# The 640-point column DFTs of a spectral filter as 10-point butterflies on VectorE and 64-point products on TensorE

## The chip, the cores and the metric

The kernel runs on one core of a Trainium2 chip. The metric is the device time of one execution in microseconds (us). Of most kernels several executions are taken, and the median is quoted with the lowest and the highest; all of these were in the fast state. e2, e3 and e7 are single runs, so their state is unknown; their times are used with care, their instruction durations more freely. The granted TensorE clock was 1.0 to within 0.002 except in e4 (0.97) and e6 (0.96 to 0.97). The span of a profile is 1.7 to 3.0 us shorter than the time of the same execution.

In the profiles PE is the matrix unit (TensorE), PEld its weight loads, DVE VectorE and ACT ScalarE. `arena` is the program's memory in SBUF, from which the matmuls read; `ps` is PSUM, into which they write. "L926" is line 926 of that kernel's source; lines shift between the kernels, so the names of the stages are given beside them.

## The reference

Shortened:

```python
def reference(A_x, A_w_r, A_w_i, B_x, B_w_gate, B_w_up, B_w_down):   # x: 1 x 2048 x 640, bf16
    def _A_ref(x, w_r, w_i):                       # w_r, w_i: 2048 x 321
        X = rfft2(x.astype(float32)) * (w_r + 1j * w_i)
        return irfft2(X, s=(S, D)).astype(bfloat16)
    def _B_ref(x, w_gate, w_up, w_down):           # 640 x 1536, 640 x 1536, 1536 x 640
        return ((x @ w_gate) * (x @ w_up)) @ w_down
    xn = _layernorm(A_x, axis=-1)
    return A_x + _A_ref(xn, A_w_r, A_w_i) + _B_ref(xn, B_w_gate, B_w_up, B_w_down)
```

So there is a layernorm, then two branches on its result: a gated network, and a filter in the two-dimensional frequency domain. The sum of both and the input is the output.

## The kernel before

The program is a list of small tasks, each with an engine, a price in ns and a priority. A planner simulates the engines with these prices when the kernel is built, and fixes the order of instructions on each engine. Each engine then runs its list in order; before's trace shows it at 107.02 us, where a gate product on DVE had waited 0.27 us for ACT, and CB (L935), whose operands WM had finished at 106.76, ran only after it, at 107.23. A price that is wrong changes nothing in the work, only in the order.

The stages, each done for 16 blocks or tiles of 128 rows:

- **LN**: layernorm of a 128 x 640 block; statistics, subtraction and scale on DVE. The block is transposed on PE.
- **GU, eG, H**: the gated products (ten matmuls a unit), their eviction on ACT, and the product gate times up on DVE. They depend only on LN and fill PE wherever the filter waits.
- **L1, L2**: the folds that cut the 640-point column DFT into even and odd, cosine and sine halves, on DVE.
- **R**: first half of the 2048-point row DFT. **D**: the column DFT, with the folded cosine and sine matrices. **C**: second half of the row DFT (complex, four matmuls).
- **WM, CB**: the spectral product with the weights (DVE, PSUM times SBUF), and its combination into real and imaginary part.
- **IA, IB**: first half of the inverse row DFT. **I**: the inverse column DFT. **U1, U2**: its unfolding on DVE.
- **ACC, FIN**: down-projection, with the second half of the inverse row DFT as a thirteenth matmul into the same sum; then the addition of the input on DVE, and the store.

The parts that the argument touches (prices, dependencies and the first lines of the functions cut, comments added):

```python
# D: the column DFT of one tile
for h in range(2):
    c.e.matmul(ps[:, bk + h, 0:320], v_uq[:, 4, t, :], v_fd[:, 640 + 320 * h: 960 + 320 * h], start=True, stop=False)
    for g in (2 * h, 2 * h + 1):
        o = (g % 2) * 160
        ins = c.e.matmul(ps[:, bk + h, o:o + 160], v_uq[:, g, t, :], v_fd[:, g * 160:(g + 1) * 160],
                         start=False, stop=(g % 2 == 1))
# WM: the spectral product. p (fp32) = x (PSUM, fp32) * weights (SBUF, bf16); e = even or odd column
x4 = ps[:, bk:bk + 2, 0:_LP].rearrange("p c (e m) -> p c e m", e=2)
for w in range(2):
    wv = v_w[:, wr, w, :].rearrange("p (m e) -> p e m", e=2)
    wv = wv.unsqueeze(1).to_broadcast([128, 2, 2, 161])
    ins = c.e.tensor_tensor(v_p[:, r2, w, :, :].rearrange("p c (m e) -> p c e m", e=2), x4, wv, _OP.mult)
# CB
c.e.tensor_tensor(v_y[:, r2, 0, :], v_p[:, r2, 0, 0, :], v_p[:, r2, 1, 1, :], _OP.subtract)
c.e.tensor_tensor(v_y[:, r2, 1, :], v_p[:, r2, 0, 1, :], v_p[:, r2, 1, 0, :], _OP.add)
```

The innermost loop of WM runs over m. In SBUF the weights are then read at every second bf16 (a step of 4 bytes) and the product is written at every second fp32 (8 bytes).

Of the kernel before, what the change touches and what calls it, by code (L numbers as in the profile page):

```python
# [70 lines left out]
class _Sched(object):  # L71
# [81 lines left out]
    def plan(self, nbanks=8, filler_deadline=0.0):  # L153
# [56 lines left out]
        while nsch < ntot:  # L210
            cands = []
            for t in avail:
# [14 lines left out]
                for ei, e in enumerate(t.engs):  # L227
                    est = eng_free[e]
                    for d in t.deps:
                        lat = _SLAT[e] if d.eng == e and not d.nbytes else _XLAT[e]  # L230
                        de = d.end + lat
                        if de > est:
                            est = de
                    if bank_ready > est:
                        est = bank_ready
                    fin = est + t.dur[e]
                    score = fin + (self.affinity if ei > 0 else 0.0)
                    if best is None or score < best[3]:
                        best = (est, fin, e, score)
# [153 lines left out]
def _build_tables():  # L393
# [25 lines left out]
    dd = np.arange(160) + 0.5  # L419
    lset = (np.arange(0, 320, 2), np.arange(1, 321, 2), np.arange(2, 322, 2), np.arange(1, 321, 2))  # L420
    full = []
    for g in range(4):
        ang = two_pi * dd[:, None] * lset[g][None, :] / _D
        full.append(np.cos(ang) if g < 2 else -np.sin(ang))
    fd = np.zeros((128, 4 * 160 + 640), np.float64)
    for g in range(4):
        fd[:, g * 160:(g + 1) * 160] = full[g][0:128]
        fd[g * 32:(g + 1) * 32, 640 + g * 160:640 + (g + 1) * 160] = full[g][128:160]
    t["fd"] = _bf16_bits(fd)

    gd = np.zeros((128, 4 * 160 + 640), np.float64)
    ml = np.arange(128)
    for g in range(4):
        l_ = 2 * ml + (g % 2)
        cl = np.where((l_ == 0) | (l_ == 320), 1.0, 2.0) / _D
        ang = two_pi * l_[:, None] * dd[None, :] / _D
        gd[:, g * 160:(g + 1) * 160] = cl[:, None] * (np.cos(ang) if g < 2 else -np.sin(ang))
        l_ = 256 + 2 * np.arange(33 if g % 2 == 0 else 32) + (g % 2)
        cl = np.where(l_ == 320, 1.0, 2.0) / _D
        ang = two_pi * l_[:, None] * dd[None, :] / _D  # L440
        v = cl[:, None] * (np.cos(ang) if g < 2 else -np.sin(ang))
        if g == 0:
            v[32] = 0.0
        gd[l_ - 256, 640 + g * 160:640 + (g + 1) * 160] = v
# [11 lines left out]
    ti = np.zeros((128, 16, 2, 256), np.float64)  # L456
    for tt in range(16):
# [18 lines left out]
        ti[:, tt, 0, 0:128] = im.real.T  # L476
        ti[:, tt, 0, 128:256] = im.imag.T
        ti[:, tt, 1, 0:128] = -im.imag.T
        ti[:, tt, 1, 128:256] = im.real.T
# [21 lines left out]
_CHUNKS = ((0, 1), (1, 1), (2, 1), (3, 1), (4, 2), (6, 2), (8, 2), (10, 2), (12, 2), (14, 2))  # L501
_LP = 322
# [36 lines left out]
def _build(nc, A_x, A_w_r, A_w_i, B_w_gate, B_w_up, B_w_down, out, opts=None):  # L539
# [3 lines left out]
    with es:  # L543
# [8 lines left out]
        sch.caps = {"glu": opts.get("cap_glu", 2), "acc": opts.get("cap_acc", 3), "fill": 1}  # L552
# [17 lines left out]
        b_w = alloc("W", _NW * 2 * _LP)  # L570
        b_z2 = alloc("Z2", 3 * 2 * 2048)
        b_x = alloc("X", 16 * 640, at=lay["Z2"][0])
        b_tf = alloc("TF", 16 * 3 * 128)
        b_ti = alloc("TI", 16 * 512)
        b_wd = alloc("WD", 12 * 640, at=lay["TI"][0])
        b_fd = alloc("FD", 1280)
        b_g = alloc("G", 1280)
# [3 lines left out]
        b_dum = alloc("DUM", 256)  # L581
        o_r = cur[0]

        b_l = alloc("L", 2 * 1280)
        b_f = alloc("F", 3 * 640)
# [4 lines left out]
        b_y = alloc("Y", 2 * 2 * _LP)  # L590
        o_end = max(o_end, cur[0])
        cur[0] = o_r
        b_tc = alloc("TC", 2 * 640)
        b_pm = alloc("PM", 2 * 1280)
# [18 lines left out]
        v_v = V("V").rearrange("p (a d) -> p a d", a=16)  # L613
        v_w = V("W").rearrange("p (r w l) -> p r w l", r=_NW, w=2)
        v_z2w = V("Z2").rearrange("p (tc a t m) -> p tc a t m", tc=6, a=16, t=16)
        v_z2 = V("Z2").rearrange("p (t c a n) -> p t c a n", t=3, c=2, a=16)
        v_x = V("X").rearrange("p (r d) -> p r d", r=16)
        v_tf = V("TF").rearrange("p (t m k) -> p t m k", t=16, m=3)
# [5 lines left out]
        v_gbf = V("GBF").rearrange("p (r n) -> p r n", r=6)  # L624
        v_dum = V("DUM")
        v_l = V("L").bitcast(_F32).rearrange("p (r c d) -> p r c d", r=2, c=2)
        v_ff = V("F").rearrange("p (r n) -> p r n", r=3)
        v_fm = v_ff[:, :, 0:512].rearrange("p r (g d) -> p r g d", g=4)
        v_fr = v_ff[:, :, 512:640].rearrange("p r (g d) -> p r g d", g=4)
        v_a = V("A").rearrange("p (r n) -> p r n", r=3)  # L630
        v_p = V("P").bitcast(_F32).rearrange("p (r w c l) -> p r w c l", r=2, w=2, c=2)
        v_y = V("Y").rearrange("p (r c l) -> p r c l", r=2, c=2)
        v_tc = V("TC").bitcast(_F32).rearrange("p (r c d) -> p r c d", r=2, c=2)
        v_pm = V("PM").bitcast(_F32).rearrange("p (r s c d) -> p r s c d", r=2, s=2, c=2)
# [8 lines left out]
        v_rs = SF(448, 16)  # L643
        v_mv = arena[:, o_stat + 384: o_stat + 416].rearrange("p (b k) -> p b k", b=16)
# [5 lines left out]
        b_rs = sch.buf("rs", 10 ** 9 + 20, 1)  # L650
        b_sd = sch.buf("sd", 10 ** 9 + 30, 1)
# [29 lines left out]
        dma("ld_fd", v_fd, d_fd, 128 * 2560, [(b_fd, None)], prio=0.3)  # L681
# [3 lines left out]
        dma("ld_g", v_g, d_g, 128 * 2560, [(b_g, None)], prio=0.36)  # L685
# [33 lines left out]
        for gi, (b0, nb) in enumerate(_LN_GROUPS):  # L719
            pbase = (1.0 if gi < 4 else 5.4) + 0.05 * gi  # L720
            for b in range(b0, b0 + nb):
                def em_bn(c, b=b):
                    c.e.bn_stats(v_st[:, b, 0:6], v_x[:, b, 0:320])  # L723
                    return c.e.bn_stats(v_st[:, b, 6:12], v_x[:, b, 320:640])
                T("bn%d" % b, "dve", 800.0, em_bn, reads=[(b_x, ("s", b, b + 1))],
                  writes=[(b_st, ("b", b, b + 1))], prio=pbase)

                def em_ag(c, b=b):
                    return c.e.bn_aggr(v_mv[:, b, :], v_st[:, b, :])
                T("ag%d" % b, "dve", 130.0, em_ag, reads=[(b_st, ("b", b, b + 1))],  # L730
                  writes=[(b_mv, ("b", b, b + 1))], prio=pbase)
# [15 lines left out]
            for b in range(b0, b0 + nb):  # L747
# [7 lines left out]
                def em_mul(c, b=b):  # L755
                    return c.e.tensor_scalar(v_x[:, b, :], v_x[:, b, :], v_rs[:, b:b + 1], None, _OP.mult)
                muls[b] = T("mul%d" % b, "dve", 290.0, em_mul, reads=[(b_rs, ("b", b, b + 1))],
# [21 lines left out]
        for b in range(16):  # L779
            lr = b % 2  # L780
            fr = b % 3
            pf = 6.0 + 0.05 * b

            def em_l1(c, b=b, lr=lr):
                c.e.tensor_tensor(v_l[:, lr, 0, :], v_x[:, b, 0:320], v_x[:, b, 639:319:-1], _OP.add)
                return c.e.tensor_tensor(v_l[:, lr, 1, :], v_x[:, b, 0:320], v_x[:, b, 639:319:-1], _OP.subtract)  # L786
            T("L1_%d" % b, "dve", 2 * _d_dve(320), em_l1, after=[muls[min(b + 6, 15)]],
              reads=[(b_x, ("s", b, b + 1))],
              writes=[(b_l, ("r", lr, lr + 1))], prio=pf)

            def em_l2(c, lr=lr, fr=fr):
                ins = None
                for v_, lo, n in ((v_fm, 0, 128), (v_fr, 128, 32)):
                    c0 = v_l[:, lr, :, lo:lo + n]
                    c1 = v_l[:, lr, :, 319 - lo:319 - lo - n:-1]
                    c.e.tensor_tensor(v_[:, fr, 0:4:3, :], c0, c1, _OP.add)  # L796
                    ins = c.e.tensor_tensor(v_[:, fr, 1:3, :], c0, c1, _OP.subtract)  # L797
                return ins
            T("L2_%d" % b, "dve", 2 * _d_dve(256) + 2 * _d_dve(64), em_l2, reads=[(b_l, ("r", lr, lr + 1))],
              writes=[(b_f, ("r", fr, fr + 1))], prio=pf)  # L800

            def em_r(c, fr=fr):
                bk = bank_of(c.t)
                ins = None
                for j in range(5):
                    st = v_ff[:, fr, j * 128:(j + 1) * 128]
                    ins = c.e.matmul(psflat[:, bk * 512 + j * 128: bk * 512 + (j + 1) * 128], st, v_sm[:, 1, :],  # L807
                                     start=True, stop=True)
                return ins
            tr = T("R_%d" % b, "pe", 5 * _d_mm(128), em_r, reads=[(b_f, ("r", fr, fr + 1)), (b_sm, None)],  # L810
                   prio=pf, bank="pair", cls="a")

            def em_er(c, b=b, tr=tr):
                bk = bank_of(tr)
                src = psflat[:, bk * 512: bk * 512 + 640].rearrange("p (j t m) -> p j t m", j=5, t=16)
                return copy_on(c, v_u[:, :, :, b, :], src)
# [50 lines left out]
        def em_az(c):  # L867
            return c.e.memset(V("A"), 0.0)
# [259 lines left out]
```

## Time and profile before

| | before |
|---|---|
| time, median of 3 | 223.83 us (223.77 to 223.86) |
| span of the profile, granted clock | 221.8 us, 1.0 |
| busy: PE, DVE, ACT | 216.7, 162.2, 112.0 us |
| first D, first ACC matmul | 85.10, 160.78 us |

The first forward column matmul (D) and the first matmul of the accumulation (ACC) split the run into three parts: about 85 us in which layernorm and folds prepare all blocks, about 76 us in which the spectrum is made and inverted, and about 61 us of accumulation. These two marks are used for all kernels below. The prediction shows the page and the groups of before. One more view matters later, DVE in order of time in the spectral part: start, time until the last of the group has ended, engine, line, operation, tiles and shapes.

```profile
105.20 1.56 DVE L926 TENSOR_TENSOR arena<-ps,arena 128x644 f32<-128x644 f32 x2
107.02 0.29 DVE L859 TENSOR_TENSOR arena<-arena 128x256 bf16<-128x256 bf16 x1 [0.27 <-ACT arena L677]
...
108.04 1.56 DVE L926 TENSOR_TENSOR arena<-ps,arena 128x644 f32<-128x644 f32 x2
```

A tile of the spectral part takes 2.84 us (105.20 to 108.04), and DVE still has 0.27 us over in it: the bracket says that it waited for an eviction on ACT.

### The profile page before, as it was taken

What the parts mean: (1) busy time and instruction counts of PE and PEld (TensorE: products, weight loads), DVE (VectorE), ACT (ScalarE), POOL (GpSimd) and SP (SyncE); (2) the same over time, 40 slices, a digit from 0 to 9 for tenths busy, and PEclk for the clock granted to TensorE, in tenths of its full rate; (3) what the DMA queues carried; (4) which work ended last, traced back from release to release, by engine and by line L of the source; (5) the groups of instructions that cost most, each with busy time, mean ns of one, the idle gap of its engine ahead of it and who ended that gap; (6) DMA issues with size and microseconds to landing.
All of it is one profiled execution on the core that took longest, in us unless ns stands there. A gap on an engine that the chain in (4) does not pass through costs nothing.

```text
span 221.8 us, 5449 instructions
## 1 busy us (share of the span) xinstructions
PE 216.7 (98%) x2204; PEld 184.3 (83%) x2204; DVE 162.2 (73%) x481; ACT 112.0 (50%) x225; POOL 0.2 (0%) x4
## 2 busy tenths in 40 slices
PE   8999999999999999999999999999999999999995
PEld 8988999999999998888888898888867777777773
DVE  3779999999999994999999958998994222222321
ACT  2576888677777777777777566556520000000000
POOL 0000000000000000000000000000000000000000
DMA  7999995000000000232232029200002332323211
GB/s 197 303 345 392 413 371 92 3 4 0 0 3 0 4 0 3 46 65 62 63 67 55 7 85 317 77 0 3 0 15 78 102 98 79 106 86 106 77 44 44
DMA packets 22184, 21.16 MB, mean 95 GB/s; under 512 B 2192, under 2 KB 21008, under 8 KB 21904
## 3 DMA queue, kind: packets, MB, share of 16 engines
q1 hardware_dynamic: 20048, 19.74, 29.5%
q10 hardware_dynamic: 2112, 1.08, 1.9%
q8 instruction: 17, 0.28, 0.5%
q14 instruction: 7, 0.06, 0.1%
HBM read 18.19 MB, written 2.62 MB: 94 GB/s over the span
## 4 chain that ended last, share of the span: by engine, by line
PE 87%; DMA 4%; DVE 3%; SPq 3%; issue 1%; ACT 0%
PE ps L844 43%; PE ps L1030 23%; DMA arena<-in_A_x_dram 4%; PE ps L945 3%; SPq L671 3%; PE ps L807 2%; PE ps L891 2%; PE ps L887 2%; PE ps L1032 2%; PE ps L985 2%; PE ps L989 2%; PE ps L764 2%; PE ps L962 2%; PE ps L913 1%; PE ps L914 1%; PE ps L912 1%
## 5 line engine op out<-in xcount | busy, mean ns | idle before, releaser
L677 ACT ACTIVATE arena<-ps 128x512 bf16<-128x512 f32 (+5 forms) x214 | 109.3, 543 | 47.0 <-PE ps L844 37.7
L844 PE MATMUL ps<-arena 128*128 128x256 bf16 (+1 forms) x1200 | 115.5, 251 | 0.6 <-ACT arena L677 0.5
L844 PEld LDWEIGHTS ps<-arena 128*128 128x128 bf16 x1200 | 96.1, 98 | 9.1 <-issue 0.7
L1030 PE MATMUL ps<-arena 128*128 128x320 bf16 x384 | 56.6, 299 | 0.0
L1030 PEld LDWEIGHTS ps<-arena 128*128 128x128 bf16 x384 | 37.5, 98 | 14.5
L1039 DVE TENSOR_TENSOR arena<-ps,arena 128x320 bf16<-128x320 f32 x32 | 15.7, 491 | 37.2 <-PE ps L1032 37.2
L859 DVE TENSOR_TENSOR arena<-arena 128x256 bf16<-128x256 bf16 (+1 forms) x120 | 30.9, 258 | 11.9 <-ACT arena L677 9.6
L926 DVE TENSOR_TENSOR arena<-ps,arena 128x644 f32<-128x644 f32 x32 | 24.9, 819 | 1.3 <-PE ps L915 1.3
L723 DVE BATCH_NORM_STATS2 arena<-arena 128x6 f32<-128x320 bf16 x16 | 7.8, 485 | 4.5 <-DMA arena<-in_A_x_dram 4.5
L796 DVE TENSOR_TENSOR arena<-arena 128x256 bf16<-128x256 f32 (+1 forms) x32 | 10.2, 318 | 0.0
L797 DVE TENSOR_TENSOR arena<-arena 128x256 bf16<-128x256 f32 (+1 forms) x32 | 10.2, 317 | 0.0
L985 PE MATMUL ps<-arena 66*128 66x320 bf16 x32 | 9.3, 301 | 0.6 <-DVE arena L1013 0.6
L945 PE MATMUL ps<-arena 128*128 128x256 bf16 x64 | 9.6, 273 | 0.0
L1032 PE MATMUL ps<-arena 128*128 128x320 bf16 x32 | 9.6, 299 | 0.0
L989 PE MATMUL ps<-arena 128*128 128x160 bf16 x64 | 9.3, 231 | 0.0
L891 PE MATMUL ps<-arena 128*128 128x160 bf16 x64 | 9.1, 233 | 0.0
L887 PE MATMUL ps<-arena 128*128 128x320 bf16 x32 | 9.1, 299 | 0.0
L1004 DVE TENSOR_TENSOR arena<-ps,arena 128x320 f32<-128x320 f32 x16 | 7.8, 485 | 0.3
L935 DVE TENSOR_TENSOR arena<-arena 128x322 bf16<-128x322 f32 x16 | 7.8, 487 | 0.1
L1012 DVE TENSOR_TENSOR arena<-arena 128x320 bf16<-128x320 f32 x16 | 7.7, 484 | 0.1
L936 DVE TENSOR_TENSOR arena<-arena 128x322 bf16<-128x322 f32 x16 | 7.8, 486 | 0.0
L786 DVE TENSOR_TENSOR arena<-arena 128x320 f32<-128x320 bf16 x16 | 7.7, 483 | 0.0
(45 smaller groups left out, 157.9 us busy)
## 6 DMA issues: line engine op xcount, KB each, us to landing
arena<-in_A_x_dram SPq DMA_DIRECT2D x20, 160.0 KB, 2.3
out_dram<-arena SPq DMA_DIRECT2D x32, 80.0 KB, 1.6
arena<-c_ti SPq DMA_DIRECT2D x1, 2048.0 KB, 18.1
arena<-in_B_w_down_dram SPq DMA_DIRECT2D x1, 1920.0 KB, 9.2
arena<-c_tf SPq DMA_DIRECT2D x4, 384.0 KB, 11.6
arena<-in_A_w_r_dram SPq DMA_DIRECT2D x32, 40.1 KB, 2.2
arena<-in_A_w_i_dram SPq DMA_DIRECT2D x32, 40.1 KB, 2.3
arena<-in_B_w_gate_dram SPq DMA_DIRECT2D x4, 320.0 KB, 7.7
```

What stands on the lines that cost most here:

```text
L677: return c.e.activation(dst, src, _ACTF.Copy)
L844: ins = c.e.matmul(ps[:, bk, w * n:(w + 1) * n], v_gw[:, w, j, ft, :], v_xt[:, j, rows], start=(j == 0), stop=(j == 4))
L859: return c.e.tensor_tensor(v_ht[:, ft, rows], v_gbf[:, rr, 0:n], v_gbf[:, rr, n:2 * n], _OP.mult)
L887: c.e.matmul(ps[:, bk + h, 0:320], v_uq[:, 4, t, :], v_fd[:, 640 + 320 * h: 960 + 320 * h], start=True, stop=False)
L891: ins = c.e.matmul(ps[:, bk + h, o:o + 160], v_uq[:, g, t, :], v_fd[:, g * 160:(g + 1) * 160], start=False, stop=(g % 2 == 1))
L926: ins = c.e.tensor_tensor(v_p[:, r2, w, :, :].rearrange("p c (m e) -> p c e m", e=2), x4, wv, _OP.mult)
L945: ins = c.e.matmul(ps[:, bk, lt * 256:(lt + 1) * 256], v_y[:, r2, cc, lt:256:2], v_ti[:, t, cc, :], start=(cc == 0), stop=(cc == 1))
L985: c.e.matmul(ps[:, bk + h, 0:320], v_z2[0:66, 2, h, a, :], v_g[0:66, 640 + 320 * h: 960 + 320 * h], start=True, stop=False)
L989: ins = c.e.matmul(ps[:, bk + h, e * 160:(e + 1) * 160], v_z2[:, e, h, a, :], v_g[:, g * 160:(g + 1) * 160], start=False, stop=(e == 1))
L1030: c.e.matmul(ps[:, bk, 0:320], v_ht[:, ft, a * 128:(a + 1) * 128], v_wd[:, ft, sl3], start=(ft == 0), stop=False)
L1032: return c.e.matmul(ps[:, bk, 0:320], v_sm[:, 2, :], v_v[:, a, sl3], start=False, stop=True)
L1039: return c.e.tensor_tensor(v_out[:, a % 2, sl3], ps[:, bk, 0:320], v_xr[:, xs, sl3], _OP.add)
```

## The change

The intent is to take work from PE, which bounds the kernel (busy for 216.7 of 221.8 us). A 640-point DFT splits into 10 x 64. The 10-point part is done as real butterflies on DVE, for two blocks at a time; the 64-point part is a dense product, and five matmuls of about 128 columns do what two of 320 and four of 160 did. The same is done backwards after the inverse row DFT. As DVE gets more work, the statistics of eight of the sixteen layernorm blocks go to ACT, the gate products are done for two units at once, and a sign copy for the inverse goes to ACT. The output columns of D now come in classes of l modulo 10, so WM meets the weights in that order.

The core of the diff, with cuts in brackets and some lines joined:

```diff
+            def em_s1(c, b=b, gr=gr):            # forward butterflies, S1 to S5, for two blocks
+                uo = v_us[:, gr].rearrange("p (u o) j b -> p o u j b", u=2)
+                for o, op in ((0, _OP.add), (1, _OP.subtract)):
+                    c.e.tensor_tensor(uo[:, o, :, 0:3, :], v_xb[:, b:b + 2, 0:6:2, :], v_xb[:, b:b + 2, 5:10:2, :], op)
+                    ins = c.e.tensor_tensor(uo[:, o, :, 3:5, :], v_xb[:, b:b + 2, 6:10:2, :], v_xb[:, b:b + 2, 1:5:2, :], op)
     ... (S2: two of 512; S3, S4, S5: eight of 256, some of them:)
+                c.e.scalar_tensor_tensor(v_f4[:, gr, 0, :, 1, :], m2, _RT, m1, _OP.mult, _OP.add)
+                c.e.scalar_tensor_tensor(v_ys, v_tw[:, 0], -0.25, u0, _OP.mult, _OP.add)
     ... (D)
-                for h in range(2):
-                    c.e.matmul(ps[:, bk + h, 0:320], v_uq[:, 4, t, :], v_fd[:, 640 + 320 * h: 960 + 320 * h],
-                               start=True, stop=False)
-                    for g in (2 * h, 2 * h + 1): ...
+                for k in range(5):
+                    n = 128 if k < 4 else 130
+                    ins = c.e.matmul(psflat[:, bk * 512 + k * 128: bk * 512 + k * 128 + n], v_uq[:, k, t, :],
+                                     v_fd[:, k * 128: k * 128 + n], start=True, stop=True)
     ... (WM)
-                x4 = ps[:, bk:bk + 2, 0:_LP].rearrange("p c (e m) -> p c e m", e=2)
-                for w in range(2):
-                    wv = v_w[:, wr, w, :].rearrange("p (m e) -> p e m", e=2)
-                    ...
+                for h in range(2):
+                    xh = ps[:, bk:bk + 2, 0:256].rearrange("p c (k h m) -> p h c k m", k=4, h=2)[:, h]
+                    wv = v_w[:, wr, :, 0:320].rearrange("p w (m k) -> p w k m", k=10)
+                    wv = wv[:, :, 1:5, :] if h == 0 else wv[:, :, 9:5:-1, :]
+                    for w in range(2):
+                        c.e.tensor_tensor(
+                            v_p[:, r2, w, :, 0:256].rearrange("p c (k h m) -> p h c k m", k=4, h=2)[:, h], xh,
+                            wv[:, w].unsqueeze(1).to_broadcast([128, 2, 4, 32]), _OP.mult)
+                ins = c.e.tensor_tensor(
+                    v_p[:, r2, :, :, 256:321], ps[:, bk:bk + 2, 256:321].unsqueeze(1).to_broadcast([128, 2, 2, 65]),
+                    v_w[:, wr, :, 0:321:5].unsqueeze(2).to_broadcast([128, 2, 2, 65]), _OP.mult)
     ... (CB in four parts, the sign copy NG on ACT; IA and IB become ten matmuls of 128)
     ... (inverse butterflies V1 to V5 in place of U1, U2; ACC and its thirteenth matmul become two tasks)
     ... (statistics of blocks 8 to 15 with two ACT passes with accumulated output)
```

> **What bounds the kernel now.** I read the page's engine totals and slices first, then the PE groups by shape, then PE's waits, then the time-ordered view, for start-to-start times.
>
> ```profile
> PE 216.7 (98%) x2204; PEld 184.3 (83%) x2204; DVE 162.2 (73%) x481; ACT 112.0 (50%) x225; POOL 0.2 (0%) x4
> ...
> PE   8999999999999999999999999999999999999995
> ...
> DVE  3779999999999994999999958998994222222321
> ACT  2576888677777777777777566556520000000000
> ...
> PE 87%; DMA 4%; DVE 3%; SPq 3%; issue 1%; ACT 0%
> ```
>
> PE is busy to the end and makes 87% of the chain. DVE is nearly full in slices 4 to 31, though, and only the last nine slices (output accumulation) leave it idle. PE's waits sum to 2.3 us, so PE work is what counts while the others keep up:
>
> ```profile
> L945 PE MATMUL ps<-arena 128*128 128x256 bf16 x64 | 9.6, 273 | 0.0
> L989 PE MATMUL ps<-arena 128*128 128x160 bf16 x64 | 9.3, 231 | 0.0
> L985 PE MATMUL ps<-arena 66*128 66x320 bf16 x32 | 9.3, 301 | 0.6 <-DVE arena L1013 0.6
> L891 PE MATMUL ps<-arena 128*128 128x160 bf16 x64 | 9.1, 233 | 0.0
> L887 PE MATMUL ps<-arena 128*128 128x320 bf16 x32 | 9.1, 299 | 0.0
> L807 PE MATMUL ps<-arena 128*128 128x128 bf16 x80 | 7.1, 219 | 0.0
> L962 PE MATMUL ps<-arena 128*66 128x256 bf16 x32 | 6.1, 272 | 0.0
> ```
>
> These are the column DFTs forward (L887, L891), inverse (L985, L989), the row inverse between them (L945, L962), and a 128-wide row DFT to compare. Means are latencies of overlapping matmuls. The price is the start-to-start time: five 128-wide take 0.28 us (56 ns each); ten 256-wide 1.09; twelve 320-wide 1.63 (136 ns).
>
> DVE, from the groups by shape:
>
> ```profile
> L926 DVE TENSOR_TENSOR arena<-ps,arena 128x644 f32<-128x644 f32 x32 | 24.9, 819 | 1.3 <-PE ps L915 1.3
> L859 DVE TENSOR_TENSOR arena<-arena 128x256 bf16<-128x256 bf16 x72 | 20.7, 288 | 10.6 <-ACT arena L677 8.7
> L1039 DVE TENSOR_TENSOR arena<-ps,arena 128x320 bf16<-128x320 f32 x32 | 15.7, 491 | 37.2 <-PE ps L1032 37.2
> L785 DVE TENSOR_TENSOR arena<-arena 128x320 f32<-128x320 bf16 x16 | 7.7, 483 | 0.0
> L796 DVE TENSOR_TENSOR arena<-arena 128x256 bf16<-128x256 f32 x16 | 6.7, 418 | 0.0
> ```
>
> The reader should see 37.2 us of DVE idle under the accumulation (L1039). In time order a DVE op with fp32 on a side costs, start to start, 0.14 us for 64 elements, 0.34 for 256, 0.40 for 320, 0.74 for 644: 0.07 us + 1.04 ns per element, which gives 0.47 for 384 and 0.60 for 512. A bf16 product takes 0.135 for 128 and 0.21 for 256, so 0.35 for 512.
>
> [...]
>
> **The change part by part.** PE, start to start:
> - Forward DFT per tile: two 320 and four 160 wide, 0.547 us (three tiles in 85.10 to 86.74), become five about 128 wide, 0.28. Sixteen: -4.3.
> - Inverse DFT per tile: 0.555 (two in 132.99 to 134.10) becomes 0.28. -4.4.
> - Row inverse: 0.44 + 0.22 becomes ten of 128, 0.56. -1.5.
> - The gated products: 480 of 128 and 720 of 256 become 240 and 840: 13.4 becomes 13.1, -0.3.
> Sum -10.5 us; transposes, row DFTs, the spectral product (322 to 321) and accumulation are unchanged.
>
> DVE, start to start:
> - Forward butterflies per pair of blocks: two of 384, two of 256, two of 512, eight of 256: 0.94 + 0.68 + 1.20 + 2.72 = 5.54, times 8 = 44.3. The old folds: 2 x (0.40 + 0.34 + 0.14) = 1.76, times 16 = 28.2. +16.1.
> - Inverse butterflies per pair: eight of 256, two of 512, then 640, 384, 256: 5.47, times 8 = 43.8, against 16 x 1.60 = 25.6. +18.2.
> - Spectral product and combination: 1.70 + 0.96 against 1.48 + 0.80 per tile, times 16: +6.1.
> - Gate products in pairs: 12 x 0.21 + 42 x 0.35 = 17.2 against 21.6: -4.4.
> - Half the statistics leave: 8 x 0.93, less small copies, one scale and the dropped zeroing: -7.9.
> Sum about +28 us, to 190.
>
> ACT gains eight pairs of 640-element passes (about 0.75 us each, 12) and the sign copies (about 0.56 per tile, 9); it had half its time free.
>
> Now the path, with the instruction order of the built program. **Up to the first forward DFT**, PE holds 240 small and 490 large gated matmuls, against 480 and 350: 13.4 + 53.5 = 66.9 instead of 65.0. Before got there at 85.10, so after gets there at 87.0 with the same early waits. DVE must do there: layernorm 18.7 (eight statistics 7.4, 31 subtractions or scales at 0.30, small ones 2.0), butterflies 44.3, gate products 10.9, one eviction 0.4: 74.3. It starts at 3.66 (first input block), and I allow 2.5 for waiting on inputs and 5 for same-engine waits (0.12 each where the trace shows one) and ACT: 85.5. It fits, barely.
> **From there to the last matmul** PE holds 4.5 + 8.8 + 9.0 + 4.5 + 35 x 1.09 + 32 x 1.766 = 121.5. The same sum for before is 133.8 and its trace took 134.1, so the sum is trustworthy where nothing stalls. 87.0 + 121.5 = 208.5; the tail after the last matmul was 2.6, and the clock-to-span difference 2.0: 213.1.
> **In the accumulation** the inverse butterflies now interleave. DVE per pair: 5.47 + 4 x 0.40 = 7.1; PE per pair: 4 x 1.766 + 0.56 = 7.6. It fits, by 7%.
> I add 1.5: small stalls in the spectral stage, where PE, DVE (2.66 per tile plus half a us of gate product) and ACT (estimated 2.6) all stand near 3.0 us per tile, and the down-projection weights below.
>
> **The rivals.**
> [...]
> DVE as bound through order alone: the engines are in order, a gate product that waits on ACT holds back a butterfly. For it: DVE has 1.5 us of slack before the first DFT, and L859 already waits 10.6 us. 217 to 220.
> A new transfer wait: the 1.9 MB of down-projection weights still wait for the last row inverse, 9.2 us to landing. Before left 29 us between (132 to 160.8); after leaves 7 gated units and six inverse tiles, 7.6 + 1.7 = 9.3, against 0.7 + 9.2. Costs about 0.6, included above.
> Nothing gained because PE was not the bound: its 2.3 us of waits speak against it.
>
> **Range and chances.** 213.1 + 1.5 = 214.6. The low end has no stalls and better early overlap, 210.5; the high end has DVE late by 7, 221.5. Below 219.4 counts as faster: 0.79. [...]the order rival most of same, 0.13.
>
> **What would show it.** PE busy near 206 with five 128-wide matmuls in 0.28 us; the first forward DFT near 87; first accumulation near 149; DVE near 190 and busy to the end; a 256-element scalar_tensor_tensor near 0.42 us[...]; under 1 us on the down-projection load. PE waits on DVE above 4 us before the first DFT, or on the inverse butterflies in the accumulation, would make me wrong.

Cut from the prediction are a paragraph of figures that no trace of this case shows, and one rival with its two mentions further down: that a scalar_tensor_tensor would be slower than a tensor_tensor of the same size. It was called the main risk, because before's trace holds no such instruction. No term of the forecast's sum goes with the cuts: it came to 213.1 + 1.5 = 214.6. The chances were 0.79 for faster, 0.13 for same and 0.08 for slower, most of the last for the rival that is cut. The times for ACT (0.75 us a pass, 0.56 a tile for the sign copies, 2.6 a tile in all) are the author's estimates. Before's trace has 0.70 us for an ACT pass of 640 elements, 0.60 for 512 (0.50 from start to start, 106.39 to 106.89) and 0.38 for 256; after's has 0.76 and 0.85 for the two new passes, and 0.61 for the sign copies of a tile (104.00 to 104.61).

## The result, and the profile after

| | before | after | predicted |
|---|---|---|---|
| time, median | 223.8 us (223.71 to 223.86, 4 runs) | 224.72 us (224.16 to 224.85, 4 runs) | 214.6 (210.5 to 221.5) |
| PE busy | 216.7 | 210.5 | 206 |
| DVE busy | 162.2 | 197.7 | 190 |
| first D | 85.10 | 86.16 | 87.0 |
| first ACC | 160.78 | 159.39 | near 149 |

The ratio of after to before is 1.0037, with a 95% interval of 1.0019 to 1.0054. A ratio here is the mean time of one kernel's fast runs over that of the other's fast runs of the same rounds, so it is not quite the ratio of the medians. The change is worth nothing, and the prediction is 10 us too low, outside its range.

The marks place the loss at once. The first D comes 0.8 us earlier than predicted, and the first ACC about 10 us later. From there to the end of the span 63.3 us pass, against a predicted 62 (213.1 less 2.0 less 149). So 10 us went astray in the spectral part, between the two marks.

The page after, the lines that answer to those of before: totals, DVE's slices, and the chain that ended last, by engine and by line.

```profile
PE 210.5 (95%) x2116; PEld 173.0 (78%) x2116; DVE 197.7 (89%) x535; ACT 129.4 (58%) x292; POOL 0.2 (0%) x4
...
DVE  3699999999999992999999999976999999999631
...
PE 50%; DVE 42%; DMA 2%; ACT 2%; issue 1%; SPq 0%; DVEq 0%
PE ps L923 24%; PE ps L1141 20%; DVE arena L1000 14%; DVE arena L938 3%; DVE arena L1018 3%; DVE arena L1003 2%; DMA arena<-in_A_x_dram 2%; DVE arena L1022 2%; PE ps L1068 2%; ACT arena L704 2%; PE ps L1149 2%; PE ps L813 1%; PE ps L884 1%; DVE arena L798 1%; DVE arena L837 1%
```

DVE went from 3% to 42% of the chain. The third entry of the second line names one DVE line with 14% of the span: L1000, four of the five products of WM. DVE groups by shape, columns count, then busy time and mean ns of one, then idle time before them:

```profile
L1000 DVE TENSOR_TENSOR arena<-ps,arena 128x256 f32<-128x256 f32 x64 | 35.0, 613 | 0.0
L1003 DVE TENSOR_TENSOR arena<-ps,arena 128x260 f32<-128x260 f32 x16 | 7.1, 441 | 0.0
L1018 DVE TENSOR_TENSOR arena<-arena 128x256 bf16<-128x256 f32 x16 | 6.8, 425 | 0.2
L864 DVE SCALAR_TENSOR_TENSOR arena<-arena 128x256 f32<-128x256 f32 x8 | 3.4, 420 | 0.0
```

All four handle about 256 elements per partition. Three take 420 to 441 ns, L1000 takes 613. DVE in order of time for one tile:

```profile
107.62 2.21 DVE L1000 TENSOR_TENSOR arena<-ps,arena 128x256 f32<-128x256 f32 x4
109.72 0.45 DVE L1003 TENSOR_TENSOR arena<-ps,arena 128x260 f32<-128x260 f32 x1
110.07 0.44 DVE L938 TENSOR_TENSOR arena<-arena 128x512 bf16<-128x512 bf16 x1
110.41 0.44 DVE L1018 TENSOR_TENSOR arena<-arena 128x256 bf16<-128x256 f32 x1
...
111.01 0.44 DVE L1022 TENSOR_TENSOR arena<-arena 128x256 bf16<-128x256 f32 x1
111.35 2.20 DVE L1000 TENSOR_TENSOR arena<-ps,arena 128x256 f32<-128x256 f32 x4
```

The two left out are the 65-element parts of CB, 0.14 each. No bracket with a wait stands behind any of them: DVE works without a break, and a tile takes 3.73 us (107.62 to 111.35) where before took 2.84. The four products take 2.10 us, 0.526 each from start to start, instead of the predicted 0.34. PE's waits (line, what it waited for, total us, times, longest):

```profile
PE ps L923 <- DVE arena L1003: 2.7, 6, 0.6
PE ps L1041 <- DVE arena L1003: 1.9, 5, 0.4
```

L1003 is the last product of a tile, so what PE waits for is that WM is done and its PSUM banks are free. The waits are small, though. How 10 us come out of them is seen in stretches of time (columns: stretch, length, then busy us of PE, PEld, DVE, ACT, POOL, then the clock, the DMA share and GB/s). First before, then after, from the first D to 133 us:

```profile
85.10:133.00 47.90, 47.89 (x439) 41.05 (x437) 41.50 (x83) 34.87 (x66) 0.00 (x0) 1.00 0.23 52
```

```profile
86.20:133.00 46.80, 41.16 (x428) 32.52 (x426) 44.88 (x118) 35.33 (x93) 0.00 (x0) 1.00 0.18 40
```

PE had 0.01 us idle in that stretch before and has 5.6 after; another 1.3 lie between 133 and the first ACC. The other part is hidden inside "busy": a 128-wide matmul that follows closely costs 56 ns, one that stands alone is drawn with its whole 0.22 us. PE busy is 4.5 us above the predicted 206. 5.6 + 1.3 + 4.5 is 11.4, against the 10.4 by which the mark is late. This sum sets a measured kernel against a predicted one and closes only roughly; e5 below gives a sum between two measured ones.

The theory was then: **A**, the weights of L1000 are read at every tenth bf16, a step of 20 bytes, and DVE pays for that step; the 10 us are nothing but this. The rivals: **B**, the short inner runs (32 elements) or the many-dimensional pattern cost, whatever the step; **C**, the price is real but the loss comes from the planner's order, which was made with the wrong price.

### The profile page after: what moved, and what is told of

It reads as the page before. It is cut to its first block, busy times and chain, and to the rows that moved or that the text cites. A ratio compares the mean times of both kernels' runs of the same rounds, so it can differ in the third digit from the quotient of the medians.

```text
span 222.7 us, 5325 instructions
## 1 busy us (share of the span) xinstructions
PE 210.5 (95%) x2116; PEld 173.0 (78%) x2116; DVE 197.7 (89%) x535; ACT 129.4 (58%) x292; POOL 0.2 (0%) x4
## 4 chain that ended last, share of the span: by engine, by line
PE 50%; DVE 42%; DMA 2%; ACT 2%; issue 1%; SPq 0%; DVEq 0%
PE ps L923 24%; PE ps L1141 20%; DVE arena L1000 14%; DVE arena L938 3%; DVE arena L1018 3%; DVE arena L1003 2%; DMA arena<-in_A_x_dram 2%; DVE arena L1022 2%; PE ps L1068 2%; ACT arena L704 2%; PE ps L1149 2%; PE ps L813 1%; PE ps L884 1%; DVE arena L798 1%; DVE arena L837 1%
## 5 line engine op out<-in xcount | busy, mean ns | idle before, releaser
L923 PEld LDWEIGHTS ps<-arena 128*128 128x128 bf16 x1080 | 93.3, 98 | 14.7 <-DVE arena L1003 3.7
L1141 PE MATMUL ps<-arena 128*128 128x320 bf16 x384 | 56.7, 299 | 0.0
L1141 PEld LDWEIGHTS ps<-arena 128*128 128x128 bf16 x384 | 37.3, 98 | 14.2
L1000 DVE TENSOR_TENSOR arena<-ps,arena 128x256 f32<-128x256 f32 x64 | 35.0, 613 | 0.0
L938 DVE TENSOR_TENSOR arena<-arena 128x512 bf16<-128x512 bf16 (+1 forms) x54 | 20.9, 389 | 7.3 <-ACT arena L704 7.2
L1041 PE MATMUL ps<-arena 128*128 128x128 bf16 x80 | 10.7, 219 | 2.7 <-DVE arena L1003 1.9
L1041 PEld LDWEIGHTS ps<-arena 128*128 128x128 bf16 x80 | 7.6, 97 | 5.9 <-ACT arena L704 3.1
L1042 PE MATMUL ps<-arena 128*128 128x128 bf16 x80 | 10.6, 219 | 0.0
L1149 PE MATMUL ps<-arena 128*128 128x320 bf16 x32 | 9.6, 299 | 0.0
L837 DVE TENSOR_TENSOR arena<-arena 128x384 f32<-128x384 bf16 x16 | 8.9, 554 | 0.0
L1042 PEld LDWEIGHTS ps<-arena 128*128 128x128 bf16 x80 | 7.8, 98 | 0.0
L1003 DVE TENSOR_TENSOR arena<-ps,arena 128x260 f32<-128x260 f32 x16 | 7.1, 441 | 0.0
L1018 DVE TENSOR_TENSOR arena<-arena 128x256 bf16<-128x256 f32 x16 | 6.8, 425 | 0.2
L813 PE MATMUL ps<-arena 128*128 128x128 bf16 x80 | 6.3, 219 | 0.6 <-ACT arena L704 0.4
L757 ACT ACTIVATE arena<-arena 128x640 bf16<-128x640 bf16 x8 | 6.8, 846 | 0.0
L1022 DVE TENSOR_TENSOR arena<-arena 128x256 bf16<-128x256 f32 x16 | 6.8, 422 | 0.0
L838 DVE TENSOR_TENSOR arena<-arena 128x256 f32<-128x256 bf16 x16 | 6.7, 421 | 0.0
```

The costliest lines, as they stand in the source:

```text
L923: ins = c.e.matmul(ps[:, bk, w * n:(w + 1) * n], v_gw[:, w, j, ft, :], v_xt[:, j, rows], start=(j == 0), stop=(j == 4))
L938: return c.e.tensor_tensor(v_ht[:, ft0:ft0 + 2, rows], v_gbf[:, rr, :, 0:n], v_gbf[:, rr, :, n:2 * n], _OP.mult)
L1000: c.e.tensor_tensor(v_p[:, r2, w, :, 0:256].rearrange("p c (k h m) -> p h c k m", k=4, h=2)[:, h], xh, wv[:, w].unsqueeze(1).to_broadcast( ...
L1003: ins = c.e.tensor_tensor(v_p[:, r2, :, :, 256:321], ps[:, bk:bk + 2, 256:321].unsqueeze(1).to_broadcast([128, 2, 2, 65]), v_w[:, wr, :, 0 ...
L1018: c.e.tensor_tensor(ym[:, :, 2, :], k4(p01), k4(p10), _OP.add)
L1022: return c.e.tensor_tensor(ym[:, :, 1, :], k4(p00), k4(p11), _OP.subtract)
```

## The experiments

### e1: the weights read at unit stride (wrong result on purpose)

```diff
-                    wv = v_w[:, wr, :, 0:320].rearrange("p w (m k) -> p w k m", k=10)
-                    wv = wv[:, :, 1:5, :] if h == 0 else wv[:, :, 9:5:-1, :]
+                    wv = v_w[:, wr, :, 128 * h:128 * h + 128].rearrange("p w (k m) -> p w k m", k=4)
```

The wrong weights are used, everything else stays, the order of instructions too.

> The four 256-element spectral products per tile took 0.526 us start to start in the changed kernel, where I had priced 0.34; per tile 0.74 us too much, 16 tiles 11.9 us. This kernel reads the weight operand of these four products at unit stride instead of every tenth bf16 (20 bytes apart); shapes, short rows of 32, broadcast, PSUM side and output stay (results are wrong on purpose). Theory A (the 20-byte step of the weight operand costs[...]): mean 0.42 us for one product instead of 0.61, spectral stage PE-bound at about 3.0 us per tile, first accumulation near 150, total 213 to 216. Theory B (rows of only 32 elements in a three-level pattern cost a restart each, or the PSUM side does): the product stays near 0.61 us and the total near 224.7. Theory C (the product is slow by its step, but another wait, ScalarE's sign copies in the loop, takes its place): product 0.42 us, total 218 to 222.

Measured: 214.37 us (214.28 to 214.66), ratio to before 0.9577 (0.9563 to 0.9591). First D at 86.21, first ACC at 149.42. The group:

```profile
L999 DVE TENSOR_TENSOR arena<-ps,arena 128x256 f32<-128x256 f32 x64 | 22.6, 418 | 0.0
```

One operand's step is worth 10.3 us of the 224.7 (medians of different calls). The instructions have the same number of elements, the same inner runs and the same order. B and C are out as the main cause. The time is 0.2 us from the predicted 214.6, and the mark 0.4 from the predicted 149.

### e2: the price against the step (wrong result on purpose)

```diff
+                def st(s):     # wf: the weights of both parts as one row
+                    return bc(wf[:, 0:32 * s].rearrange("p (m k) -> p k m", k=s)[:, 0:4, :])
+                c.e.tensor_tensor(po(0, 0), xs(0), st(6), _OP.mult)
+                c.e.tensor_tensor(po(0, 1), xs(0), st(7), _OP.mult)
+                c.e.tensor_tensor(po(1, 0), xs(1), st(8), _OP.mult)
+                c.e.tensor_tensor(po(1, 1), xs(1), st(16), _OP.mult)
```

> The same four products per tile, each with another step of the weight operand: 6, 7, 8 and 16 bf16 elements (12, 14, 16 and 32 bytes). Results wrong on purpose. Theory A[...]: 6 and 7 between 0.42 and 0.61 us[...], 8 and 16 at 0.61 or more. If it is a threshold at 16 bytes: 6 and 7 at 0.42, 8 and 16 alike and slow. Theory B: all four near 0.61 whatever the step.

Measured, one run: 221.64 us. Groups of DVE by shape, from a step of 16 bf16 (L1011) over 8 and 7 down to 6 (L1008):

```profile
L1011 DVE TENSOR_TENSOR arena<-ps,arena 128x256 f32<-128x256 f32 x16 | 9.8, 611 | 0.0
L1010 DVE TENSOR_TENSOR arena<-ps,arena 128x256 f32<-128x256 f32 x16 | 9.8, 609 | 0.0
L1009 DVE TENSOR_TENSOR arena<-ps,arena 128x256 f32<-128x256 f32 x16 | 8.8, 553 | 0.0
L1008 DVE TENSOR_TENSOR arena<-ps,arena 128x256 f32<-128x256 f32 x16 | 8.0, 497 | 0.0
```

From 16 bytes on a longer step costs no more: 32 bytes (611), 20 bytes (613, after) and 16 bytes (609) are alike. Below it the price falls: over the 418 of the dense group the step costs 191 ns at 16 bytes, 135 at 14 and 79 at 12. A's expectation holds, and a sharp threshold at 16 bytes is refuted, since 12 and 14 bytes cost too. L1003, with 260 elements at a step of 10 bytes, took 432 to 441 over the runs with the order of after, 10 to 19 more than an estimated 422 (418 and 4 x 1.04). Only this dependence on the step is shown; the mechanism behind it is not.

### e3: which operand pays (wrong result on purpose)

Lines are joined and comments added in this cut:

```diff
+                # wf: weights as one row, w4 = wf[:, 0:320] as (m k) with k = 10; bc: broadcast over both parts
+                c.e.tensor_tensor(pu(0, 0).rearrange("p c (m k) -> p c m k", k=4), x0.rearrange("p c (k m) -> p c m k", k=4),
+                                  bc(wf[:, 0:128].rearrange("p (m k) -> p m k", k=4)), _OP.mult)      # L1005: PSUM stepped
+                c.e.tensor_tensor(pu(0, 1).rearrange("p c (k m) -> p c m k", k=4), x1.rearrange("p c (m k) -> p c m k", k=4),
+                                  bc(wf[:, 128:256].rearrange("p (m k) -> p m k", k=4)), _OP.mult)    # L1008: output stepped
+                c.e.tensor_tensor(pu(1, 0).rearrange("p c (k m) -> p c m k", k=4), x0.rearrange("p c (k m) -> p c m k", k=4),
+                                  bc(w4[:, :, 1:5]), _OP.mult)                 # L1011: weights in fours, PSUM and output stepped
+                c.e.tensor_tensor(pu(1, 1).rearrange("p c (m k) -> p c m k", k=4), x1.rearrange("p c (m k) -> p c m k", k=4),
+                                  bc(w4[:, :, 9:5:-1]), _OP.mult)              # L1013: weights in fours, rest dense
```

"Stepped" is a step of 32 fp32, 128 bytes. "In fours" is four neighbouring weights, then the next four ten further on: inner runs of 4 instead of 32.

> Which operand a wide step costs on. Four products per tile: first, weights and output dense, PSUM walked with a step of 32 fp32 (128 bytes); second, weights and PSUM dense, output written with a step of 128 bytes; third, weights in runs of four adjacent elements, PSUM and output both with the wide step; fourth, weights in runs of four backwards, PSUM and output dense. Results wrong on purpose. If only reads from SBUF pay: first, second, third and fourth all near 0.42 us, and the order with four adjacent weights innermost is a repair. If PSUM reads pay too, first and third near 0.6; if writes pay, second and third near 0.6. If short runs cost (theory B in another form), third and fourth, with runs of four, are far slower than 0.61.

Measured, one run: 217.58 us. Groups of DVE by shape:

```profile
L1005 DVE TENSOR_TENSOR arena<-ps,arena 128x256 f32<-128x256 f32 x16 | 6.7, 418 | 0.0
L1008 DVE TENSOR_TENSOR arena<-ps,arena 128x256 f32<-128x256 f32 x16 | 9.6, 599 | 0.0
L1011 DVE TENSOR_TENSOR arena<-ps,arena 128x256 f32<-128x256 f32 x16 | 9.8, 616 | 0.0
L1013 DVE TENSOR_TENSOR arena<-ps,arena 128x256 f32<-128x256 f32 x16 | 6.7, 419 | 0.0
```

A wide step in PSUM, 128 bytes, costs nothing (418, as dense in e1). Weights in fours cost nothing (419), although the runs are shorter and go backwards: B is refuted. An output written to SBUF at a wide step costs as much as a read (599). The expectation lists this outcome, but theory A as I held it spoke of reads alone. L1011 shows that weights in fours with the output still stepped would be no repair. The first and the last line together name one: take the weights in fours, give PSUM the wide step, and write p in the order in which it comes.

### e4: the planner told the true price

```diff
-            wm = T("WM_%d" % t, "dve", 4 * _d_dve_psum(256) + _d_dve_psum(260), em_wm,
+            wm = T("WM_%d" % t, "dve", 4 * 526.0 + _d_dve_psum(260), em_wm,
```

The work is that of after, only the order of instructions differs. This is the test of C.

> The changed kernel with one number of its planner altered: the spectral product is planned at 526 ns instead of 336 ns for each of its four parts, so the static order fits what the chip does; the instructions are the same. If the loss is the static order alone (engines in order, planned with a wrong price): 216 to 219. If the price itself is the loss, VectorE has 16 x 3.7 us in the spectral stage whatever the order, and only gated products can move: 221 to 225.

Measured: 228.0 us (227.63 to 228.28), ratio to before 1.0181 (1.0164 to 1.0198), correct. All four runs had a mean granted clock of 0.97. Both expectations are missed: it is slower than after. Stretches of time (columns as above):

```profile
86.00:150.00 64.00, 62.50 (x650) 53.69 (x648) 61.05 (x161) 50.97 (x127) 0.00 (x0) 1.00 0.16 33
150.00:165.00 15.00, 8.08 (x53) 5.93 (x54) 9.25 (x24) 4.60 (x9) 0.00 (x0) 0.56 0.54 175
```

With the true price the planner fills each tile with more gated products. PE then has 1.5 us idle until 150, where after had 5.6 by 133. But the gated products are used up before the spectral part is through, and from 150 to 165 PE is busy for 8.1 of 15 us, at a granted clock of 0.56. The idle time is moved to the end and not removed, and the lower clock comes on top. So the loss does not come from a wrong order, at least not from one that this planner mends by the right price. That some other order would lose less is not excluded.

### e5: the repair, with a right result

```diff
-                    xh = ps[:, bk:bk + 2, 0:256].rearrange("p c (k h m) -> p h c k m", k=4, h=2)[:, h]
-                    wv = v_w[:, wr, :, 0:320].rearrange("p w (m k) -> p w k m", k=10)
-                    wv = wv[:, :, 1:5, :] if h == 0 else wv[:, :, 9:5:-1, :]
+                    xh = ps[:, bk:bk + 2, 0:256].rearrange("p c (k h m) -> p h c m k", k=4, h=2)[:, h]
+                    wv = v_w[:, wr, :, 0:320].rearrange("p w (m k) -> p w m k", k=10)
+                    wv = wv[:, :, :, 1:5] if h == 0 else wv[:, :, :, 9:5:-1]
     ...
-                            v_p[:, r2, w, :, 0:256].rearrange("p c (k h m) -> p h c k m", k=4, h=2)[:, h], xh,
+                            v_p[:, r2, w, :, 0:256].rearrange("p c (h m k) -> p h c m k", k=4, h=2)[:, h], xh,
     ... (CB and NG over the dense 256 elements; the row inverse takes its columns at a step of four)
+                    y1, y2 = ((v_y[:, r2, 256 + k:768:4], v_y[:, r2, k:512:4]) if k < 4 else
+                              (v_y[:, r2, 768:896], v_y[:, r2, 896:1024]))
```

The loop over the four classes k becomes the innermost. The wide step goes to PSUM. The order of p and y changes with it, and the weight load of the row inverse sorts the columns out, at a step of 8 bytes.

> A correct repair after what the step runs showed (SBUF steps of 16 bytes or more cost VectorE on the weight read and on the written output, PSUM steps do not): the products' loops run with four adjacent weights innermost, PSUM takes the wide step, and product and combination buffers are laid out in that order, so every SBUF side is dense; the row inverse then loads its stationary columns at a step of four bf16 (8 bytes). Theory A: product 0.42 us, the same time as with the false unit-stride weights, 213.5 to 215.5, correct. Rival: the stepped stationary load slows TensorE's row inverse (more than 0.56 us for ten matmuls) and takes back 1 us or more: 216 to 219.

Measured: 214.26 us (213.96 to 215.31, 5 runs), against 223.85 for before (223.65 to 224.46, 9 runs): ratio 0.9574 (0.9552 to 0.9596), correct. First D at 86.09, first ACC at 149.43. The page's totals, its chain, and the group of WM:

```profile
PE 206.5 (97%) x2116; PEld 174.4 (82%) x2116; DVE 185.8 (88%) x535; ACT 128.5 (61%) x292; POOL 0.2 (0%) x4
...
PE 74%; DVE 18%; DMA 4%; SPq 1%; ACT 1%; issue 1%; DVEq 0%
```

```profile
L1000 DVE TENSOR_TENSOR arena<-ps,arena 128x256 f32<-128x256 f32 x64 | 22.6, 415 | 0.0
```

The 64 products cost 415 ns each instead of 613, DVE is busy 11.9 us less than in after, and PE carries 74% of the chain instead of 50%. In time order a tile now takes 3.05 us in the mean of three (103.94 to 113.09), and DVE has a little idle time again (0.19 us ahead of one gate product). The ten matmuls of the row inverse still take 0.56 us (103.13 to 103.69); their weight loads with the step of 8 bytes take 112 ns instead of 98, which is hidden.

With this kernel the loss can be accounted for between two measured ones, from the first D to the first ACC. First after from 133 us on (its earlier part is shown above), then e5:

```profile
133.00:159.40 26.40, 25.12 (x262) 21.44 (x260) 23.02 (x61) 18.55 (x42) 0.00 (x0) 1.00 0.34 106
```

```profile
86.10:133.00 46.90, 46.32 (x515) 40.70 (x513) 44.47 (x146) 40.42 (x109) 0.00 (x0) 1.00 0.22 44
133.00:149.40 16.40, 16.16 (x175) 14.55 (x173) 12.06 (x33) 12.76 (x26) 0.00 (x0) 1.00 0.49 160
```

Both run 690 matmuls there. PE is idle for 6.9 us in after and for 0.8 in e5, and busy for 66.3 against 62.5. Idle time makes 6.1 us and the drawn-out "busy" 3.8, together the 9.9 by which this part is shorter.

This version beats before by 4.3% and after by 4.7% (224.72 to 214.26, medians of different calls).

### e6: e5 with all layernorm statistics on VectorE

```diff
-                if b >= opts.get("act_stats", 8):
+                if b >= opts.get("act_stats", 16):
     ... (and the same number in one more place)
```

The question is what the change's other part, the statistics on ACT, is worth.

> The repaired kernel with the other eight blocks' layernorm statistics back on VectorE. My sum put VectorE at 85.5 us before the first forward DFT against 87.0 for TensorE; eight more statistics at 0.93 us less the small copies add 6.8. If that sum is right VectorE becomes the bound there: the first forward DFT near 92 instead of 86, total 218 to 221. If VectorE's margin was larger than I thought (rival: waits I allowed for do not exist), total 214 to 216.

Measured: 226.13 us (225.33 to 226.95), ratio to before 1.0084 (1.0055 to 1.0113), correct. First D at 98.33, first ACC at 159.08. DVE is busy for 193.3 us in all, 7.5 more than in e5. PE's waits:

```profile
PE ps L1037 <- ACT arena L1025: 3.7, 2, 2.0
PE ps L1064 <- DVE arena L1096: 3.0, 1, 3.0
```

Both expectations are missed: the first D was to come near 92, the total at 218 to 221, or at 214 to 216 with more margin. Without this part the change would not pay even when repaired: it is worth 11.9 us here. That is more than I expected, and the 7.5 us of DVE work explain it only in part. The first D comes 12.2 us later. Until then PE is not idle (96.8 busy of 98.3 us, with 1086 matmuls where e5 has 967): gated products are drawn forward, and are missing later, when PE waits for the sign copies (L1025) and the inverse butterflies (L1096), at a mean clock of 0.93 in the spectral part and 0.96 after it. The planner makes a new order with every change of prices or engines, so the size of 11.9 holds for this planner. The direction is shown, the split between DVE's work and the order is not.

### e7: finer steps of writes, and ScalarE (wrong result on purpose)

Comments are added in this cut:

```diff
+                    c.e.tensor_tensor(v_p[:, r2, 0, :, 0:256].rearrange("p c (k m e) -> p e c k m", k=4, e=2)[:, h],
+                                      xh, wv[0], _OP.mult)                       # L999: fp32 written at a step of 8 bytes
+                    c.e.tensor_tensor(v_p[:, r2, 1, :, 0:256].rearrange("p c (g m e) -> p g c e m", g=2, e=4)[:, h],
+                                      xh, wv[1], _OP.mult)                       # L1001: at a step of 16 bytes
     ... (the weights at unit stride as in e1; in NG, one copy of 64 elements reads at a step of 16 bytes:)
+                c.e.activation(v_y[:, r2, 833:897].rearrange("p (k s j) -> p k s j", k=4, s=2), ym[:, :, 1:3, 0:64:8], _ACTF.Copy, scale=-1.0)
```

> Results wrong on purpose. Two of the four products write their output at a step of two fp32 (8 bytes), two at four fp32 (16 bytes), with dense weights; and one ScalarE copy of 64 elements reads SBUF at a step of 16 bytes. [...]0.42 us at 8 bytes (as the 644-wide products of the kernel before ran), about 0.61 at 16. If only a far larger write step pays: both 0.42. ScalarE: 0.24 us as with the dense source means that it does not pay; 0.29 or more that it does.

The clause cut there gave the case of the first two prices: that writes cost at the same steps as reads.

Measured, one run: 216.71 us. Groups by shape:

```profile
L1001 DVE TENSOR_TENSOR arena<-ps,arena 128x256 f32<-128x256 f32 x32 | 19.6, 613 | 0.0
L999 DVE TENSOR_TENSOR arena<-ps,arena 128x256 f32<-128x256 f32 x32 | 13.5, 423 | 0.0
```

```profile
L1029 ACT ACTIVATE arena<-arena 128x64 bf16<-128x64 bf16 x16 | 4.9, 307 | 0.0
L1030 ACT ACTIVATE arena<-arena 128x63 bf16<-128x63 bf16 x16 | 3.8, 240 | 0.0
```

A write at 16 bytes costs what a read at 16 bytes costs (613 and 609), and at 8 bytes it costs nearly nothing (423, against 418 dense). That fits before's WM, with its 4-byte reads and 8-byte writes: its 0.74 us for 644 elements lie on the line through the dense operations (0.34 for 256, 0.40 for 320), 0.07 us + 1.04 ns per element. ScalarE was slower too: 307 ns for 64 elements at 16 bytes against 240 for 63 dense ones, about 1 ns per element. But this copy also reads in runs of only 8, and no run separates the two on ScalarE; that the step is the reason there is likely, not shown.

### The runs together

For each of the kernels with the order of after, the extra DVE time per tile is the sum of its four mean times less 4 x 418. The third column is the time from the first D to the first ACC in its profile:

| kernel | extra per tile, us | D to ACC, us | time, us |
|---|---|---|---|
| after | 4 x 613: 0.78 | 73.2 | 224.72 |
| e2 | 611 + 609 + 553 + 497: 0.60 | 71.0 | 221.64 (one run) |
| e7 | 2 x 613 + 2 x 423: 0.40 | 65.5 | 216.71 (one run) |
| e3 | 418 + 599 + 616 + 419: 0.38 | 65.1 | 217.58 (one run) |
| e1 | 0 | 63.2 | 214.37 |

The stage gets longer with every addition to DVE's time, but not in proportion. From 0.78 to 0.60 it loses 2.2 us, where 16 x 0.18 is 2.9; from 0.60 to 0.40 it loses 5.5, where 16 x 0.20 is 3.2; from 0.40 to 0 only 2.3, where 16 x 0.40 is 6.4. The last step fits a stage in which PE takes over as the bound (in e5, with products as fast as e1's, PE is idle there for 0.8 us). Why the middle step is larger than DVE's own saving is not explained. Nor is it that e3 takes 0.9 us longer than e7 with a shorter stage; both are single runs.

## Why the prediction was wrong

**The step that failed** is the line "Spectral product and combination: 1.70 + 0.96 against 1.48 + 0.80 per tile, times 16: +6.1". Its second term is right: CB takes 0.33 + 0.14 + 0.14 + 0.33 from start to start, 0.94. Its first term took 0.34 for every 256-element operation, by the formula 0.07 us + 1.04 ns per element, which had been made from operations with dense operands or steps of a few bytes. The four products measured 0.526 each: 2.10 + 0.35 = 2.45 per tile, 0.75 too much, 12.0 over sixteen tiles. The diff shows the cause in plain sight, `(m k) -> k m` with k = 10 on the weights. I counted elements and did not look at the step. e1 shows that this term accounts for the miss: with dense weights the same kernel takes 214.37, and e5 with a right result 214.26, where 214.6 was predicted. No large errors cancel in that: e5 has the first D 0.9 us early, and from there to the end of the last matmul takes 123.5 us, against 121.5 and 1.5 for stalls.

**Why nearly all of it went through.** 12.0 us of DVE time cost 10.3 us of run time (e1). The prediction itself says that PE, DVE and ACT all stand near 3.0 us per tile in the spectral part, and adds 1.5 us for small stalls and the down-projection weights. That very balance made the stage the worst place for an error: little could hide 0.75 us more of DVE. The range had allowed for DVE late by 7 us, but neither of the waits that it named as signs of being wrong lies in the spectral part, where PE waited for WM (4.6 us in all).

**What was right**, as after and e5 show it:
- PE's sum of -10.5: 216.7 to 206.5 in e5. Five D matmuls take 0.28 us and the ten of the row inverse 0.56.
- The first D at 87.0: 86.16. "It fits, barely" held.
- The accumulation. DVE's inverse butterflies fit under it; PE waits for them 0.5 us once in after. The 7% of room was enough.
- DVE's other terms, less exactly: 190 was predicted, and e5, where the failed term is as priced, has 185.8. So in after 12.0 us too much in one term stood against some 4 too little elsewhere, and the total of 197.7 showed only 7.7; where the 4 us lie was not traced. The statistics can be checked: -7.9 predicted, 7.5 between e6 and e5. On ACT they had been put at 12 us and took 16.4 busy, of which 3.5 are the separate instructions that read the accumulator (226 and 217 ns each, L751 and L757 in after); the first D was not late for it.
- The first accumulation at about 149: 149.43 in e5.
- The load of the down-projection weights was put at 0.6 us. In after it cost nothing, because everything before it was late; in e5 it cost 0.3.

**The rivals.** The one that is cut, a slower scalar_tensor_tensor, is refuted: 420 ns for 256 fp32 elements (L864 in after), as for a tensor_tensor (418, L796 in before). "DVE as bound through order alone" named the right engine but the wrong place and cause: before the first D there was no loss, and in the spectral part it was price and not order (e1 keeps the order, e4 changes it). The rival that PE was not the bound in before is refuted by e5: 10.2 us less of PE work took 9.6 us off the time. The new transfer wait is as small as predicted. None of them was the cause; the cause was a price that I had not doubted.

**What stays open.** The mechanism behind the price is not shown: only steps of 10 to 32 bytes on the read side and 8, 16 and 128 on the write side were measured. How much of e6's 11.9 us is DVE work and how much is order is not settled, and whether some order of after's own instructions would lose less than 10 us is not either. Nor is it why the loss grows unevenly with DVE's extra time, or whether ScalarE pays for the step or for the short runs.

## What to carry to other kernels

When a layout changes, price each vector operation by the step of every SBUF operand and of the output, not by elements alone: in this case a product of 256 elements took 599 to 616 ns with an SBUF side at a step of 16 bytes or more, instead of 418. Only this form, bf16 weights times fp32 from PSUM into fp32, was tried. A permutation that is needed anyway belongs on the side where it was free here: PSUM reads by VectorE (418 ns at a step of 128 bytes), runs of a few neighbours (419 for runs of four), or the weight load of a matmul that comes anyway (112 ns instead of 98 at a step of 8 bytes, the ten matmuls still 0.56 us). And where three engines balance in a stage, an error in one price is multiplied by the number of tiles (here 0.75 us by 16), so that stage deserves the closest look at its instructions.
